# Sixty-four rows instead of fifty in the score products of an attention loop

## The chip, the cores and the metric

The kernel runs on one core of one Trainium2 chip. The metric is device time in microseconds (us) of one launch, here the median of three runs. The core has a matrix engine (TensorE, "PE"; its weight loads are listed apart as "PEld"), a vector engine (VectorE, "DVE"), an activation engine (ScalarE, "ACT"), GpSimd ("POOL") and SyncE ("SP"), which here only issues transfers (DMAs).

## The reference

Two mixers of the same sequence, blended by a gate. Sequence 2048, width 512, 32 heads of 16. The second mixer reads an input of its own name with the same values, so the kernel takes one `x`.

```python
g = sigmoid((x * gate_w).sum(-1, keepdims=True))
# a: full softmax attention
qkv = (x @ wqkv).reshape(B, S, 3, H, Dh).transpose(2, 0, 3, 1, 4)
scores = einsum("bhqd,bhkd->bhqk", q, k) * Dh ** -0.5
a = (softmax(scores) @ v, heads joined) @ wo
# b: Fourier mixing with given matrices, real part
b = dft_seq_re @ (x @ dft_hid_re.T) - dft_seq_im @ (x @ dft_hid_im.T)
out = g * a + (1 - g) * b
```

The weights `wqkv` and `wo` are drawn 64 times larger than usual, so the scores are large and the softmax needs the maximum of each row of scores.

## The kernel before

**Number format.** Products run in a 32-bit format of reduced mantissa (`F32R`). Where that isn't exact enough, a number is split into a high and a low part, and three products (high-high, high-low, low-high) are added. For queries and keys this is done by stacking: a head of 16 becomes 48 rows, `[k hi, k hi, k lo]` against `[q hi, q lo, q hi]`, so one product of 48 rows gives the sum of the three.

**Two heads at a time.** A pair of heads `p` (16 pairs) lies in two tiles of 128 partitions, `qs` and `ks`, each 2048 wide: head 0 of the pair in partitions 0 to 47, head 1 in 64 to 111. `row_loads` (L84) makes the pair of tiles and its eight transfers. All these tiles come from the pool `stk`, which has six buffers; a transfer into a buffer waits until its last reader is done.

**Two passes.** The *scan* computes every score once to get the row maxima: `scan` (L121, product at L130, maximum on DVE at L132) or `scan_folded` (L136, products at L149). There are 64 scan steps a pair, 1024 in all. `shift` (L158) negates and splits the maxima of a pair into two rows and stores them in DRAM (`m_d`). The *use* pass loads a pair again with `load_use` (L103): after the eight row loads it fills, for each half `j`, two more rows from partition `b = 64*j + 48` on. The rows of `ks` get ones, from the DRAM tile `ones_d`; the rows of `qs` get the two rows of negated maxima. A product over 50 rows is thus the score less its maximum, and ACT can take the exponential straight from PSUM.

**The front** (the first 695 us) does the projections, the transform along the width, most of the transform along the sequence, and beside these the first 692 scan steps. At its start it loads `xT` and the weights through SP's queue (L414 to L422), then stores the ones to `ones_d` (L429), and goes on with stores of the projected queries and keys (L383, L215). Operands of the transforms are split into tiles `b0` to `b31` of the pool `big`; `block(i)` names them, and block 31 holds the low part of the last quarter of the last row block of `x`.

**The loop** (L893 on, the last 1050 us) has 16 pairs of 32 steps. A step handles 128 keys for 1024 queries of both heads: `qk2` (L634) makes the scores of 512 queries (`c = 0`: both heads into one pair of banks `s3`, one exponential of 1024 columns, L649) and of 512 more (`c = 1`: two single banks of three, two exponentials of 512 columns, L653). In each, the two heads are two products, one on each half of the array's rows (L645). `pv` (L658) multiplies the exponentials of an earlier step with the values, four heads' parts side by side in the columns of the array (L660), into the bank `pvb`. Beside this stand:

- steps 0 to 331: one scan step each (`next_scan`), L130 and L132;
- steps 333 to 460: the rest of the transform along the sequence (`spectral`, L776). Its coefficients come through SP (`load_unit`, L765, two buffers), are split by DVE (`split_unit`, L772 and L773, two buffers of each part) and multiplied at L180;
- from step 461 on: the output projection and the blend (`mix_heads`, `take_in`, L754). From step 333 on, `pv` runs for two steps at once in every second step.

**Order.** Each engine runs its instructions in program order, written out by hand. At step 18 of a pair the loop emits `load_use` of the next pair (L898); 10 steps before a scan ends it emits the loads of the next scan. SP takes its transfers strictly one after the other. Each of them raises one of eight semaphores in turn, and waits until the transfer eight places before it has landed. The first score product of a pair waits for the transfers of its `qs` and `ks`.

Of the kernel before, what the change touches and what calls it, by code (L numbers as in the profile page):

```python
# [10 lines left out]
F32 = mybir.dt.float32  # L11
# [7 lines left out]
P = 128  # L19
S = 2048  # L20
D = 512
H = 32
DH = 16
# [23 lines left out]
def build(tc, x, xT, wqkv, wo, wrT, wiT, cr, ci, gate, out):  # L47
    nc = tc.nc
    with ExitStack() as ctx:
# [3 lines left out]
        big = ctx.enter_context(tc.tile_pool(name="big", bufs=1, reuse_waits="tile"))  # L53
        dram = ctx.enter_context(tc.tile_pool(name="dram", bufs=1, space=DRAM))
# [7 lines left out]
        y_d = [dram.tile([P, 4, D], F32, name=f"y_d{c}") for c in range(NC)]  # L62
        o_d = [[dram.tile([2, 2, NP // ND, 64, 512], F32, name=f"o_d{f}_{i}") for i in range(2)] for f in range(ND)]
        r_d = [[dram.tile([4, 512], F32, name=f"r_d{p}_{h}") for h in range(2)] for p in range(NP)]
        ones_d = dram.tile([2, S], F32, name="ones_d")

        ident = keep.tile([P, P], F32, name="ident")
        make_identity(nc, ident)
# [8 lines left out]
        gm = keep.tile([P, NB], F32, name="gm")  # L77
        ones = keep.tile([P, 32], F32, name="ones")
        nc.vector.memset(ones, 1.0)


        scanned, used, unfolded = {}, {}, {}

        def row_loads(p, queue, keys=k_d):  # L84

            qs = stk.tile([P, S], F32R, tag="stk", name="qs")
            ks = stk.tile([P, S], F32R, tag="stk", name="ks")
            loads = []
            for j in range(2):
                b, r = 64 * j, slice(DH * ((2 * p + j) % 8), DH * ((2 * p + j) % 8) + DH)  # L90
                loads += [(ks[b:b + 32, :], keys[p // 4][r, 0:1, :].to_broadcast([DH, 2, S])),
                          (qs[b:b + 32, :], q_d[p // 4][r, :, :].rearrange("e n s -> (e n) s")),
                          (ks[b + 32:b + 48, :], keys[p // 4][r, 1, :]),
                          (qs[b + 32:b + 48, :], q_d[p // 4][r, 0, :])]
            return (qs, ks), [lambda dst=dst, src=src: queue.dma_start(dst.bitcast(F32), src) for dst, src in loads]
# [7 lines left out]
        def load_use(p):  # L103
            if p < NP:
                used[p], loads = row_loads(p, nc.sync)
                for load in loads:
                    load()
                qs, ks = used[p]
                for j in range(2):
                    b = 64 * j + 48  # L110
                    nc.sync.dma_start(ks[b:b + 2, :].bitcast(F32), ones_d)
                    for n in range(2):
                        nc.sync.dma_start(qs[b + n:b + n + 1, :].bitcast(F32),
                                          m_d[p][n:n + 1, :, j].rearrange("n g b k -> n b g k"))
# [75 lines left out]
        with ExitStack() as pf:  # L190
# [126 lines left out]
            with ExitStack() as px:  # L317
# [94 lines left out]
                def load_x(c):  # L412
                    for d in range(ND):
                        nc.sync.dma_start(raws[d][:, q4[c]], xT[d * P:(d + 1) * P, q4[c]])  # L414
# [11 lines left out]
                load_x(2)  # L426
                load_cols(1, far)
                load_x(3)
                nc.sync.dma_start(ones_d.rearrange("a (b c) -> (a b) c", c=32), ones)  # L429
                gb = ep.tile([P, D], F32, tag="gb", name="gb", bufs=1)  # L430
                after(40, nc.sync.dma_start, gb, gate.to_broadcast([P, D]))

# [95 lines left out]
            with ExitStack() as py:  # L528
# [13 lines left out]
                pss, yre, early = {}, {}, {}  # L542
# [8 lines left out]
                for n, (ph, t, u) in enumerate(coef):  # L551
# [6 lines left out]
                    if n == len(coef) - 2 * NU:  # L558
                        unfolded[FRONT // SCANS], loads = row_loads(FRONT // SCANS, nc.sync)
                        for load in loads:  # L560
                            load()
                        load_use(0)
# [45 lines left out]
        with ExitStack() as pa:  # L608
# [18 lines left out]
            def bank():  # L627
                return ps2.tile([P, 512], F32, tag="s2", name="s2", bufs=3)

            def bank2():  # L630
                ps = ps2.tile([P, 2, 512], F32, tag="s3", name="s3")
                return ps, (ps[:, 0, :], ps[:, 1, :])

            def qk2(p, h, kb, c):  # L634
                n = turn[c]
                turn[c] += 1
                q0 = h * 1024 + c * 512
                qs, ks = used[p]
                if c == 0:
                    ps, pss = bank2()  # L640
                else:
                    pss = [bank() for j in range(2)]
                for j in range(2):
                    b = 64 * j
                    nc.tensor.matmul(pss[j], ks[b:b + 50, kb * P:(kb + 1) * P],  # L645
                                     qs[b:b + 50, q0:q0 + 512], start=True, stop=True)
                if c == 0:
                    e = both[n % len(both)]
                    nc.scalar.activation(e, ps, AF.Exp, scale=SCALE)  # L649
                    return [e[:, j, :] for j in range(2)]  # L650
                e = [ring[n % len(ring)] for ring in single]
                for j in (1, 0):
                    nc.scalar.activation(e[j], pss[j], AF.Exp, scale=SCALE)  # L653
                return e
# [238 lines left out]
            for step in range(NP * PERIODS):  # L893
                p, i = step // PERIODS, step % PERIODS
                h, kb = i // NB, i % NB
                now[0] = step
                if i == 18:
                    load_use(p + 1)  # L898
# [11 lines left out]
                if step >= MIX and step % 2 == 0:  # L910
                    next(fill)
                es = [qk2(p, h, kb, 0)]
                if step == 0:
                    es.append(qk2(p, h, kb, 1))
# [3 lines left out]
                if step:  # L918
                    es.append(qk2(p, h, kb, 1))
# [40 lines left out]
            c, ps = halves_[0], spread[0]  # L960
# [8 lines left out]
            c, ps = halves_[1], spread[1]  # L969
# [39 lines left out]
```

## Time and profile before

| what | value |
|---|---|
| median of three runs | 1755.48 us (1752.98 to 1757.93) |
| the profiled execution, its own time | 1751.4 us |
| its span, first to last instruction | 1749.6 us |
| mean granted TensorE clock | 0.995 |
| PE busy | 1719.9 us, 98% of the span |
| ACT busy | 1451.9 us, 83% |
| DVE busy | 1155.1 us, 66% |
| POOL busy | 712.7 us, 41% |
| transfers | 199.55 MB, mean 114 GB/s |

The profile is of one execution. A group's row gives the source line, the engine, the operation, the tiles written and read, the rows and columns of the array ("50*128"), the shape read, the count, the busy time (union) in us, the mean duration of one in ns, and the time that the engine stood idle before it with what ended that. Products overlap in the array and their ends are modelled, so the duration of one isn't the time that it takes from the next; the distance from start to start is. In a timeline a row is: start in us, length in us, engine, line, operation, tiles, count of merged instructions, and in brackets the idle time before it.

### The profile page before, as it was taken

How to read it: one execution, taken by the hardware profiler on the slowest of the kernel's cores; microseconds unless marked ns; L12 is line 12 of the kernel's file. 1: busy time of each engine (PE TensorE's matmuls, PEld its weight loads, DVE VectorE, ACT ScalarE, POOL GpSimd, SP SyncE). 2: the span in 40 equal slices, each digit the busy share in tenths (PEclk: the TensorE clock that was granted, in tenths of full speed). 3: DMA queues.
4: the chain of work that ended last, by engine and by line, in shares of the span. 5: the costliest groups of instructions: out<-in, count | busy, mean ns of one | idle time of the engine just before them, and what ended most of it. 6: DMA issues, size and time to landing. Idle time of an engine off the chain costs nothing.

```text
span 1749.6 us, 35589 instructions
## 1 busy us (share of the span) xinstructions
PE 1719.9 (98%) x13640; PEld 1021.8 (58%) x13640; DVE 1155.1 (66%) x1876; ACT 1451.9 (83%) x2384; POOL 712.7 (41%) x814
## 2 busy tenths in 40 slices
PE   8999999999999999999999999999999999999998
PEld 6887787888888887333333333333334555555554
DVE  6799999999999887666666666666664212222333
ACT  5445346888887887999999999999999888888885
POOL 3678667555556664032322323232232322322222
PEclk9999999999999999999999999999999999999999
DMA  8782666434354445433232423515313254255612
GB/s 296 254 298 79 190 201 206 121 115 117 104 154 140 139 133 120 74 59 63 58 67 56 82 40 64 95 23 99 78 35 73 64 118 90 68 141 137 177 36 100
DMA packets 126810, 199.55 MB, mean 114 GB/s; under 512 B 54016, under 2 KB 56560, under 8 KB 119728
## 3 DMA queue, kind: packets, MB, share of 16 engines
q1 hardware_dynamic: 84368, 161.02, 34.4%
q0 software_dynamic: 38496, 19.47, 5.2%
q10 hardware_dynamic: 3776, 16.78, 3.6%
q8 instruction: 107, 1.75, 0.4%
q14 instruction: 63, 0.52, 0.1%
HBM read 133.04 MB, written 63.71 MB: 112 GB/s over the span
## 4 chain that ended last, share of the span: by engine, by line
PE 89%; DMA 3%; DVE 3%; POOL 2%; issue 2%; ACT 1%; SPq 0%; DVEq 0%; ACTq 0%; POOLq 0%
PE pvb L660 28%; PE xy L180 21%; PE s L645 19%; PE s L180 8%; PE s L149 7%; PE s L130 6%; DVE mx L132 1%; DMA fa<-ks_d 1%; DMA kf_d<-fa 1%; POOL s L215 1%; DMA raws<-wqkv 0%; DMA raws<-xT 0%; POOL el L215 0%; POOL fa L215 0%; DMA abr<-ab_d 0%
## 5 line engine op out<-in xcount | busy, mean ns | idle before, releaser
L132 DVE TENSOR_REDUCE mx<-s 128x2 f32<-128x1024 f32 x524 | 627.2, 1222 | 207.5 <-PE s L130 207.4
L649 ACT ACTIVATE eb<-s 128x1024 f32<-128x1024 f32 x512 | 579.3, 1131 | 55.1 <-PE s L645 55.1
L653 ACT ACTIVATE e<-s 128x512 f32<-128x512 f32 x1024 | 610.3, 708 | 0.4 <-PE s L645 0.4
L660 PE MATMUL pvb<-e,va 128*17 128x512 f32 x2048 | 517.3, 598 | 0.0
L660 PE MATMUL pvb<-eb,va 128*17 128x512 f32 x2048 | 517.1, 598 | 0.0
L645 PE MATMUL s<-qs,ks 50*128 50x512 f32 x2048 | 428.1, 438 | 2.3 <-DVE ty L600 1.6
L645 PEld LDWEIGHTS s<-qs,ks 50*128 50x128 f32 x2048 | 212.6, 185 | 372.4 <-ACT eb L649 282.6
L155 DVE CUSTOM_DVE_ANT_0 fold<-s,fold 128x512 f32<-128x512 f32 x500 | 339.1, 690 | 39.0 <-PE s L149 19.4
L153 ACT ACTIVATE fold<-s 128x512 f32<-128x512 f32 x500 | 296.1, 602 | 70.0 <-PE s L149 43.1
L149 PE MATMUL s<-ks,qs 48*128 48x512 f32 x1000 | 223.3, 404 | 7.6 <-DVE mx L155 6.1
L130 PE MATMUL s<-ks,qs 48*128 48x512 f32 x1048 | 221.6, 396 | 3.7 <-DVE mx L132 2.5
L668 POOL DMA_DIRECT2D lc<-ob x124 | 63.1, 515 | 308.2 <-DVE ob L665 307.9
L660 PEld LDWEIGHTS pvb<-eb,va 128*17 128x17 f32 x2048 | 69.2, 96 | 190.2 <-issue 182.0
L149 PEld LDWEIGHTS s<-ks,qs 48*128 48x128 f32 x1000 | 120.9, 184 | 47.6 <-DVE mx L155 18.2
L675 POOL DMA_DIRECT2D r_d<-lc x31 | 18.1, 585 | 294.9 <-DVE lc L674 286.0
L130 PEld LDWEIGHTS s<-ks,qs 48*128 48x128 f32 x1048 | 108.3, 184 | 14.9 <-DVE mx L132 6.0
L180 PE MATMUL xy<-w,b 64*128 64x512 f32 x768 | 105.2, 392 | 0.2 <-ACT s L379 0.2
L401 ACT ACTIVATE tx<-xy 128x512 f32<-128x512 f32 x48 | 28.7, 599 | 78.6 <-PE xy L180 52.5
L754 DVE SCALAR_TENSOR_TENSOR y<-s,g,y 128x512 f32<-128x512 f32 x50 | 36.6, 748 | 76.6 <-PE s L180 76.0
L677 POOL DMA_DIRECT2D rb<-r_d x124 | 60.6, 496 | 63.0 <-DMA r_d<-lc 63.0
L180 PE MATMUL s<-b,chi 64*128 64x512 f32 x542 | 85.2, 390 | 0.3 <-ACT chi L963 0.3
L180 PEld LDWEIGHTS xy<-w,b 64*128 64x128 f32 x768 | 72.5, 186 | 17.6 <-ACT s L379 1.0
(750 smaller groups left out, 2320.4 us busy)
## 6 DMA issues: line engine op xcount, KB each, us to landing
craw<-ci SPq DMA_DIRECT2D x64, 256.0 KB
craw<-cr SPq DMA_DIRECT2D x60, 256.0 KB
ks<-k_d SPq DMA_DIRECT2D x46, 256.0 KB
qs<-q_d SPq DMA_DIRECT2D x46, 256.0 KB
ab_d<-ab SPq DMA_DIRECT2D x32, 256.0 KB
y_d<-y SPq DMA_DIRECT2D x32, 256.0 KB
o_d<-oh POOLq DMA_DIRECT2D x28, 256.0 KB, 9.8
o_d<-ol POOLq DMA_DIRECT2D x28, 256.0 KB, 11.9
```

The costliest lines, as they stand in the source:

```text
L130: nc.tensor.matmul(ps[:, j, :], qs[b:b + 48, qb * P:(qb + 1) * P], ks[b:b + 48, c * 512:(c + 1) * 512], start=True, stop=True)
L132: nc.vector.tensor_reduce(mx[p][:, :, qb, c], ps, axis=AX.X, op=ALU.max)
L149: nc.tensor.matmul(ps, qs[b:b + 48, qb * P:(qb + 1) * P], ks[b:b + 48, c * 512:(c + 1) * 512], start=True, stop=True)
L153: nc.scalar.activation(fold[j], ps, AF.Relu)
L155: nc.vector.tensor_tensor_reduce(out=fold[j], in0=ps, in1=fold[j], scale=1.0, scalar=-3.0e38, op0=ALU.add, op1=ALU.max, accum_out=mx[p][:, ...
L180: nc.tensor.matmul(ps[j], lhs[r], rhs[r], start=first, stop=last)
L645: nc.tensor.matmul(pss[j], ks[b:b + 50, kb * P:(kb + 1) * P], qs[b:b + 50, q0:q0 + 512], start=True, stop=True)
L649: nc.scalar.activation(e, ps, AF.Exp, scale=SCALE)
L653: nc.scalar.activation(e[j], pss[j], AF.Exp, scale=SCALE)
L660: nc.tensor.matmul(pvb[r:r + VC, :], va[:, kb, 2 * p + j, :], es[c][j], start=kb == 0, stop=kb == NB - 1, tile_position=(0, r))
L668: nc.gpsimd.dma_start(lc[32 * n:32 * n + 32, :], ob[r + DH:r + VC, :].rearrange("p (s e) -> p s e", e=16))
L677: nc.gpsimd.dma_start(rb[r:r + DH, :], r_d[p][h][n:n + 1, :].to_broadcast([DH, 512]))
```

## The change

The score products of the loop (L645) read 64 rows of `ks` and `qs` from partition `64*j` on, where they read 50. The 14 rows more are filled by `load_use`: in `ks` the transfer of two rows of ones becomes one of 16 rows of `ones_d`, whose last 14 are zeros; in `qs` a new transfer brings 14 rows of zeros. `ones_d` grows from 2 to 16 rows. A tile `zeros` is set to zero by DVE at the start, in the buffer of block 31, and one new transfer in the front writes it to the 14 rows.

```diff
-        ones_d = dram.tile([2, S], F32, name="ones_d")
+        ones_d = dram.tile([DH, S], F32, name="ones_d")
...
+        zeros = big.tile([112, S // 8], F32, tag="b31", name="zeros")
+        nc.vector.memset(zeros, 0.0)
...
                     b = 64 * j + 48
-                    nc.sync.dma_start(ks[b:b + 2, :].bitcast(F32), ones_d)
+                    nc.sync.dma_start(ks[b:b + DH, :].bitcast(F32), ones_d)
+                    nc.sync.dma_start(qs[b + 2:b + DH, :].bitcast(F32), ones_d[2:DH, :])
                     for n in range(2):
                         nc.sync.dma_start(qs[b + n:b + n + 1, :].bitcast(F32),
                                           m_d[p][n:n + 1, :, j].rearrange("n g b k -> n b g k"))
...
-                nc.sync.dma_start(ones_d.rearrange("a (b c) -> (a b) c", c=32), ones)
+
+                nc.sync.dma_start(ones_d[0:2, :].rearrange("a (b c) -> (a b) c", c=32), ones)
+                nc.sync.dma_start(ones_d[2:DH, :].rearrange("a (b c) -> (a b) c", c=S // 8), zeros)
...
                     b = 64 * j
-                    nc.tensor.matmul(pss[j], ks[b:b + 50, kb * P:(kb + 1) * P],
-                                     qs[b:b + 50, q0:q0 + 512], start=True, stop=True)
+                    nc.tensor.matmul(pss[j], ks[b:b + 64, kb * P:(kb + 1) * P],
+                                     qs[b:b + 64, q0:q0 + 512], start=True, stop=True)
```

`DH` is 16, `S` is 2048. The zeros add nothing to any score.

## The prediction

> **What bounds the kernel now.** I read the chain of work that ended last, then the groups that the change touches, then the busy times by stage, and last the timelines of single steps.
>
> ```profile
> PE 89%; DMA 3%; DVE 3%; POOL 2%; issue 2%; ACT 1%; SPq 0%; DVEq 0%; ACTq 0%; POOLq 0%
> ...
> L645 PE MATMUL s<-qs,ks 50*128 50x512 f32 x2048 | 428.1, 438 | 2.3 <-DVE ty L600 1.6
> L645 PEld LDWEIGHTS s<-qs,ks 50*128 50x128 f32 x2048 | 212.6, 185 | 372.4 <-ACT eb L649 282.6
> ...
> L130 PE MATMUL s<-ks,qs 48*128 48x512 f32 x1048 | 221.6, 396 | 3.7 <-DVE mx L132 2.5
> ...
> L180 PE MATMUL xy<-w,b 64*128 64x512 f32 x768 | 105.2, 392 | 0.2 <-ACT s L379 0.2
> ```
>
> PE leads the chain, and L645 stands there with 438 ns over 50 rows against 396 over 48 and 392 over 64. This looks as if 50 rows were a bad number. The trap is that this column is a modelled length of overlapping products; what counts is the distance from one pair of products to the next, and what stood before the pair. The loop has two stages:
>
> ```profile
> 720.00:1300.00 580.00, 580.00 (x4284) 218.97 (x4284) 392.45 (x365) 580.00 (x919) 176.44 (x264) 1.00 0.33 63
> 1330.00:1600.00 270.00, 270.00 (x2226) 143.86 (x2228) 57.29 (x99) 241.19 (x372) 73.75 (x110) 1.00 0.44 104
> ```
>
> The columns are the stretch, its length, busy us (with counts) of PE, PEld, DVE, ACT and POOL, the granted clock, the transfers' share and GB/s. With a scan step beside (first row) ACT is busy all the time, as PE is; later (second row) ACT has 29 us of slack in 270 and PE none. The clock is whole in both, so there is no throttle to win from. A step of the first stage:
>
> ```profile
> 902.31 0.50 PE L645 MATMUL s<-qs,ks 50*128 50x512 f32 x2
> 902.65 0.39 PE L130 MATMUL s<-ks,qs 48*128 48x512 f32 x2
> 902.85 1.24 ACT L649 ACTIVATE eb<-s 128x1024 f32<-128x1024 f32 x1
> 902.88 0.39 PE L645 MATMUL s<-qs,ks 50*128 50x512 f32 x2
> ...
> 904.20 0.50 PE L645 MATMUL s<-qs,ks 50*128 50x512 f32 x2
> 904.74 1.25 ACT L649 ACTIVATE eb<-s 128x1024 f32<-128x1024 f32 x1
> ```
>
> Here is a ring: the `c = 0` pair at 902.31, its exponential 0.54 us later, which ends at 904.09 and frees the only pair of banks, and the next `c = 0` pair at 904.20: 1.89 us a step. ACT's starts in this stage follow each other by at least 0.477 + 0.477 + 0.921 = 1.875 us, so ACT alone would allow only 0.015 us less. A step of the second stage, where PE has no gap:
>
> ```profile
> 1500.65 0.73 PE L645 MATMUL s<-qs,ks 50*128 50x512 f32 x4
> 1501.21 0.63 PE L180 MATMUL s<-b,chi 64*128 64x512 f32 x4
> 1501.68 0.40 PE L180 MATMUL s<-b,clo 64*128 64x512 f32 x2
> ...
> 1502.38 0.40 PE L180 MATMUL s<-b,clo 64*128 64x512 f32 x2
> 1502.61 0.63 PE L645 MATMUL s<-qs,ks 50*128 50x512 f32 x4
> ```
>
> Each pair, of 50 rows or 64, takes its 0.23 us, except the first after the value products (1500.65, two pairs in 0.56 us). The 0.50 us and the mean of 438 come from this place, not from the rows.
>
> **The change, part by part.**
>
> *The products.* Over all start times in the trace, the medians from a pair to the next are: a 48-row pair before a 50-row one 234 ns, 64 before 48 232, 48 before 64 235, 50 before 64 233, 64 before 50 233, 64 before 64 227 to 231. Right behind the value products the pair takes 337 ns with 50 rows, and 337 in the one place near the end where a 64-row pair stands there. Weight loads: 185 ns (50 rows), and 186 at L180 (64 rows). So a product costs by its 512 columns, and the array's half is occupied the same. There are 1024 pairs: 1024 x 0 = 0. The bounds: 50 before 50, in the odd steps of the second stage, takes 241 ns, and 64 before 64 at the least 227, so at best -14 ns a pair; on the other side the usual distances of 64-row pairs reach 237 against 230 for 50-row ones, +7 ns. On the path lie the `c = 0` pairs of the 332 scan steps (the ring) and both pairs of the other 180 steps: 332 + 360 = 692 pairs. That makes -9.7 to +4.8 us. I take 0, since the 241 stands only where the second weight load waits for ACT to free a bank.
>
> *The transfers of the loop.* Each `load_use` moves in each half 14 more rows of `ks` and 14 of `qs`, 8 KB a row: 56 rows, 448 KB, by two more transfers and two larger ones. While such loads run, the rows arrive at 104 to 216 KB per us (1548 to 1551 us), so the load takes 448/216 = 2.1 to 448/104 = 4.3 us longer; I take 3. Issue on SP is 0.4 us each, inside that. What hides it is the lead: the last row of maxima of a pair is issued 14.7 us or more before its first product (pair 0: 680.3 against 695.0; later 15.8 or more), and lands some 2 us on, by the median of the `rb` loads. Of 12.7 us, 3 are used. Pushed back behind it on SP's queue are the `yre` load and `y_d` stores at the front's end (POOL then waits 8.9 us for another tile anyway), scan loads, and in the second stage the coefficients:
>
> ```profile
> 1555.09 0.54 SPq L113 DMA_DIRECT2D qs<-m_d  x1
> ...
> 1556.95 1.06 SPq L765 DMA_DIRECT2D craw<-ci  x2
> ```
> ```profile
> 1354.67 0.43 DVE L772 CAST chi<-craw 128x512 fp32r<-128x512 f32 x1 [1.81 <-PE s L645]
> ...
> 1563.99 0.43 DVE L772 CAST chi<-craw 128x512 fp32r<-128x512 f32 x1 [5.88 <-PE s L180]
> 1564.52 0.69 DVE L773 TENSOR_TENSOR clo<-craw,chi 128x512 fp32r<-128x512 f32 x1
> ```
>
> This is the tightest cover. Casts fall every 8.74 us where PE sets them (1345.24, so 1353.98 would be due; 1555.03, so 1563.77): at both places the cast is already 0.2 to 0.7 us late, which says that the coefficient arrives just in time behind a `load_use`. Three us more go straight into DVE. But PE needs these parts only when the next block starts, at 1575.5 us for the second (the group of L180 after the one at 1571.16, 4.37 us on): 1575.5 - 1565.2 = 10.3 us of cover, and about 9.8 at the first. Of this 3 to 4.3 are used, and nothing else queues behind the cast that PE needs sooner. Cost 0. [...]
>
> *The front.* DVE's new memset of 112 x 256 lies between those of 128 x 32 (85 ns) and 128 x 512 (485 ns), so about 0.27 us, at 2.4 us, where DVE waits until 4.69 for the first `x`. The block 31 that it borrows is written only after 30 us, its transfer is read by then. The transfer itself stands on SP's queue behind `ones`, where the queue is full and PE pays:
>
> ```profile
> 19.80 0.32 SPq L215 DMA_DIRECT2D ks_d<-s  x1
> ...
> 25.85 0.73 PE L180 MATMUL xy<-b,w 64*128 64x512 f32 x4 [1.41 <-DVE b L282]
> ```
>
> The store of 19.80 lands at 24.38; DVE stands behind it, and PE behind DVE. The new transfer has 112 packets of 1 KB; such packets took 48 ns there, on 16 engines 112 x 48 / 16 = 0.34 us, and each later transfer waits for a neighbour one place on. From 0 to 0.34 + 2.75 (the longest step between two issues there, 22.45 to 25.20): I take 0.5.
>
> *Waits at the start of a pair.* L645 has 64 semaphore instructions of 51 ns, four a pair. The new count of 16 transfers behind eight semaphores changes them by one or two a pair at most: +-1.6 us, taken as 0.
>
> **Sum:** 0 + 0 + 0.5 + 0 on the profiled 1751.4 us is 1751.9. That execution lies 4.1 us under the median of 1755.5, so the forecast against the median is **1756.0 us**, no change that can be told (0.3%, or 5.3 us, is about what a measurement of this kernel can tell from no change). Its own range, with a few ns a pair either way and the front's bounds, is 1752 to 1760.
>
> **Rivals.**
>
> *A. The full half is faster.* If 227 ns holds for every pair in place of 241, 692 x 14 ns = 9.7 us, so 1746. For it: the 241, and the ring and PE leave no other slack. Against it: all mixed distances are 232 to 235, and ACT caps the ring at 0.015 us a step. Chance 0.17.
>
> *B. More rows cost PE time* (the other side). If the array takes 10 ns longer for 64 rows, the same 692 pairs cost 6.9 us, 1763. It counts as slower from 7.7 ns a pair on. For it: 237 and 235 are the longest usual distances. Against it: 48 to 64 rows within 3 ns. Chance 0.12.
>
> *C. Late coefficients.* If the two new transfers took as long as the `ks_d` store (4.59 us) and the two larger ones 1.3 more, `load_use` grows by 11.8 us; over 9.8, PE waits (11.8 - 9.8) at four places: 8 us, 1764. It decides from a growth of 9.8 us and is slower than 0.3% from 11.1. For it: the casts that are late already. Against it: measured rates. Chance 0.11.
>
> **How the numbers follow.** Forecast 0.60, A 0.17, B 0.12, C 0.11. So faster 0.17, within 0.3% 0.60, slower 0.23. The range 1748 to 1763 takes in the forecast's own, the nearer part of A, and B.
>
> **What would show it.** Right: L645 with 64 rows at 0.23 us from pair to pair and still 0.34 behind the value products; 1.89 us a step; coefficient casts behind a `load_use` some 3 us later with PE unmoved. A mean that falls from 438 with the distances unchanged would say nothing. Wrong: a ring under 1.88 us or odd steps shorter by 0.02 (A); pairs at 0.24 or more (B); PE at L180 idle, released by DVE `clo` L773 (C); PE idle at 25 us by more than 2 us (front).

## The result and the profile after

| | before | after |
|---|---|---|
| median of six runs, us | 1756.89 (1752.98 to 1758.38) | 1769.18 (1766.42 to 1771.85) |
| profiled execution, us | 1751.40 | 1768.51 |
| its span, us | 1749.6 | 1766.7 |

The changed kernel takes 1.0077 times as long, with a 95% interval of 1.0063 to 1.009: by this ratio 13.5 us more (the medians of the table lie 12.3 apart). No change had been forecast, and 1769.18 lies above the range given. In the profiled executions it is 17.1 us. Line numbers are two to five higher than before: L645 is now L650, L674 is L679, L130 and L132 are L133 and L135, L180 is L183.

From the page of the changed kernel, the shares of the chain of waits and three of the groups:

```profile
PE 83%; DMA 7%; DVE 4%; POOL 2%; issue 2%; ACT 1%; SPq 0%; DVEq 0%; ACTq 0%; POOLq 0%
PE pvb L665 25%; PE xy L183 22%; PE s L650 16%; PE s L183 8%; PE s L152 7%; PE s L133 6%; DMA lc<-ob 5%; DVE mx L135 2%; DMA raws<-xT 1%; POOL lc L673 1%; POOL s L218 1%; POOL el L218 0%; DMA fa<-ks_d 0%; DVE ob L670 0%; DMA abr<-ab_d 0%
...
L650 PE MATMUL s<-qs,ks 64*128 64x512 f32 x2048 | 428.3, 438 | 2.3 <-DVE ty L605 1.6
L650 PEld LDWEIGHTS s<-qs,ks 64*128 64x128 f32 x2048 | 207.0, 185 | 375.3 <-ACT eb L654 275.0
...
L133 PE MATMUL s<-ks,qs 48*128 48x512 f32 x1048 | 223.4, 398 | 18.2 <-DVE mx L135 17.0
```

The product that was changed is as it was: 438 ns and 428 us, with 64 rows as with 50. What is new stands beside it. DMA went from 3% to 7% of the chain, and 5% is one small transfer, `lc<-ob`; the scan product L133 has 18.2 us of idle PE ahead of it where it had 3.7, nearly all put down to DVE's maxima. The loop's two stages, in the columns of the prediction (busy PE, PEld, DVE, ACT and POOL, clock, transfers' share, GB/s):

```profile
720.00:1300.00 580.00, 566.53 (x4138) 205.71 (x4138) 378.51 (x351) 561.73 (x887) 170.44 (x256) 0.99 0.38 71
1330.00:1600.00 270.00, 270.00 (x2208) 140.57 (x2208) 62.33 (x100) 242.92 (x376) 74.82 (x108) 1.00 0.43 101
```

In the second stage PE still has no gap (270.00 us busy of 270). In the stage with scans PE lost 13.5 us in 580, ACT 18, and the clock is a little short of whole. So the loss lies there. The waits of that stretch (total us, times, longest), before:

```profile
DVE lc L674 <- DMA lc<-ob: 2.3, 5, 0.8
PEld s L130 <- DVE mx L132: 0.3, 1, 0.3
```

and after:

```profile
DVE lc L679 <- DMA lc<-ob: 20.4, 9, 4.8
PEld s L133 <- DVE mx L135: 15.7, 7, 4.3
PE s L133 <- DVE mx L135: 13.4, 6, 3.9
```

At the end of a half of a pair, DVE copies the sums into `ob` (L670), POOL gathers the row sums into `lc` by four small transfers (L673, 64 bytes a piece), and seven steps later DVE takes their reciprocal (L679). DVE waits for this gather in the kernel before too, but in this stretch for 0.8 us at most; now up to 4.8. One such place in DVE's timeline (start, length, and in brackets the idle time ahead with what ended it), before:

```profile
772.23 1.23 DVE L132 TENSOR_REDUCE mx<-s 128x2 f32<-128x1024 f32 x1 [0.66 <-PE s L130]
773.67 0.25 DVE L674 RECIPROCAL lc<-lc 128x16 f32<-128x16 f32 x1 [0.20 <-DMA lc<-ob]
774.12 1.23 DVE L132 TENSOR_REDUCE mx<-s 128x2 f32<-128x1024 f32 x1 [0.20 <-PE s L130]
```

and after, with PE's timeline of the same place under it:

```profile
769.45 1.23 DVE L135 TENSOR_REDUCE mx<-s 128x2 f32<-128x1024 f32 x1 [0.65 <-PE s L133]
773.66 0.25 DVE L679 RECIPROCAL lc<-lc 128x16 f32<-128x16 f32 x1 [2.98 <-DMA lc<-ob]
773.83 1.16 DVE L135 TENSOR_REDUCE mx<-s 128x2 f32<-128x1024 f32 x1
```
```profile
772.45 0.51 PE L650 MATMUL s<-qs,ks 64*128 64x512 f32 x2
775.04 0.50 PE L133 MATMUL s<-ks,qs 48*128 48x512 f32 x2 [2.09 <-DVE mx L135]
```

The maxima of the scan that should follow at about 771.3 stand behind the reciprocal on DVE until 773.83. PE's next scan product needs the banks that they free, and stands until 775.04; behind it stand the score products, and the ring. The chain of waits of the changed kernel, in order of time, says what the reciprocal waited for:

```profile
757.51 0.70 DVE ob L670
...
758.49 1.52 POOL lc L673 x3
760.01 13.52 DMA lc<-ob
...
773.66 0.25 DVE lc L679
773.91 1.09 DVE mx L135
775.04 0.50 PE s L133 x2
```

The gather is issued at 760.01 and lands 13.5 us on. Where no load runs beside it, 1.7 us from the last issue to the reciprocal is enough (1716.64 to 1718.30, at the end). Beside it here, on SP's queue:

```profile
754.50 0.56 SPq L97 DMA_DIRECT2D ks<-k_d  x1
...
762.49 0.30 SPq L113 DMA_DIRECT2D ks<-ones_d  x1
763.71 0.31 SPq L114 DMA_DIRECT2D qs<-ones_d  x1
...
770.60 1.36 SPq L116 DMA_DIRECT2D qs<-m_d  x2
```

This is the `load_use` with the added rows, over the whole time of the gather. The tiles for these rows come free at the end of a pair; in this stage such a load falls at the start of pairs 1, 3, 5, 7 and 9, when POOL gathers the sums of the second half of the pair before. (In the middle of the even pairs such a load and a gather meet too; the waits there are 0.9, 0.3, 1.2 and 0.5 us.) On POOL's own queue two stores of 256 KB stand ahead of the gather:

```profile
749.73 0.88 POOL L696 DMA_DIRECT2D o_d<-oh  x1
750.60 0.82 POOL L696 DMA_DIRECT2D o_d<-ol  x1
```

At the five places the second of them lands 17.3 to 18.6 us after its issue before the change and 18.0 to 19.9 after it, so at most a part of the gather's delay comes through the stores. From its last issue to its landing the gather takes 10.5 to 11.3 us at these places before and 13.3 to 15.3 after. Beside the load of a scan, which the change leaves as it was (start of pairs 2, 4, 6 and 8), it takes 9.5 to 9.8 and 9.2 to 10.1 us; with no load beside it (middle of pairs 1 to 9, the odd ones) 2.7 to 3.7 and 1.6 to 2.9.

At the five places of the two profiled executions:

| start of pair | DVE's wait ahead of the reciprocal, before, us | after, us | lost there, us | granted clock then halved |
|---|---|---|---|---|
| 1 | 0.2 | 3.0 | 3.8 | yes |
| 3 | 0.3 | 3.3 | 2.6 | no |
| 5 | 0.0 | 2.8 | 3.7 | yes |
| 7 | 0.8 | 4.8 | 5.5 | yes |
| 9 | 0.6 | 3.6 | 4.4 | yes |

"Lost" is how much the distance between the two executions grew over the place, by the starts of the exponentials of L654. The five make 20.0 us. Up to the loop the changed kernel's execution was ahead by 2.8 us (the one before has a dip of the clock of 6.8 us at 696), and 20.0 - 2.8 = 17.2 is the distance at the end. It is 17.1 at step 320 and 17.2 at step 511: the second stage gives and takes nothing.

### The profile page after: what moved, and what is told of

Its sections match the earlier page's. It is cut to its first block, busy times and chain, and to the rows that moved or that the text cites. A ratio compares the mean times of both kernels' runs of the same rounds, so it can differ in the third digit from the quotient of the medians.

```text
span 1766.7 us, 35624 instructions
## 1 busy us (share of the span) xinstructions
PE 1723.5 (98%) x13640; PEld 1016.2 (58%) x13640; DVE 1152.8 (65%) x1877; ACT 1452.7 (82%) x2384; POOL 711.4 (40%) x814
## 3 DMA queue, kind: packets, MB, share of 16 engines
q1 hardware_dynamic: 86288, 168.48, 36.4%
## 4 chain that ended last, share of the span: by engine, by line
PE 83%; DMA 7%; DVE 4%; POOL 2%; issue 2%; ACT 1%; SPq 0%; DVEq 0%; ACTq 0%; POOLq 0%
PE pvb L665 25%; PE xy L183 22%; PE s L650 16%; PE s L183 8%; PE s L152 7%; PE s L133 6%; DMA lc<-ob 5%; DVE mx L135 2%; DMA raws<-xT 1%; POOL lc L673 1%; POOL s L218 1%; POOL el L218 0%; DMA fa<-ks_d 0%; DVE ob L670 0%; DMA abr<-ab_d 0%
## 5 line engine op out<-in xcount | busy, mean ns | idle before, releaser
L135 DVE TENSOR_REDUCE mx<-s 128x2 f32<-128x1024 f32 x524 | 626.2, 1221 | 206.3 <-PE s L133 206.1
L654 ACT ACTIVATE eb<-s 128x1024 f32<-128x1024 f32 x512 | 569.5, 1112 | 60.5 <-PE s L650 60.4
L658 ACT ACTIVATE e<-s 128x512 f32<-128x512 f32 x1024 | 599.8, 688 | 11.2 <-PE s L650 11.2
L650 PE MATMUL s<-qs,ks 64*128 64x512 f32 x2048 | 428.3, 438 | 2.3 <-DVE ty L605 1.6
L650 PEld LDWEIGHTS s<-qs,ks 64*128 64x128 f32 x2048 | 207.0, 185 | 375.3 <-ACT eb L654 275.0
L133 PE MATMUL s<-ks,qs 48*128 48x512 f32 x1048 | 223.4, 398 | 18.2 <-DVE mx L135 17.0
L152 PE MATMUL s<-ks,qs 48*128 48x512 f32 x1000 | 228.0, 404 | 7.4 <-DVE mx L158 6.1
L673 POOL DMA_DIRECT2D lc<-ob x124 | 63.0, 515 | 293.4 <-DVE ob L670 293.0
L133 PEld LDWEIGHTS s<-ks,qs 48*128 48x128 f32 x1048 | 108.7, 184 | 32.2 <-DVE mx L135 23.4
L183 PE MATMUL xy<-w,b 64*128 64x512 f32 x768 | 105.3, 392 | 0.2 <-ACT s L382 0.2
L183 PE MATMUL s<-b,chi 64*128 64x512 f32 x542 | 85.7, 391 | 0.3 <-ACT chi L968 0.3
L183 PEld LDWEIGHTS xy<-w,b 64*128 64x128 f32 x768 | 72.5, 186 | 17.5 <-ACT s L382 1.0
## 6 DMA issues: line engine op xcount, KB each, us to landing
o_d<-ol POOLq DMA_DIRECT2D x28, 256.0 KB, 12.8
```

Of the source, the lines that this page charges most:

```text
L133: nc.tensor.matmul(ps[:, j, :], qs[b:b + 48, qb * P:(qb + 1) * P], ks[b:b + 48, c * 512:(c + 1) * 512], start=True, stop=True)
L135: nc.vector.tensor_reduce(mx[p][:, :, qb, c], ps, axis=AX.X, op=ALU.max)
L152: nc.tensor.matmul(ps, qs[b:b + 48, qb * P:(qb + 1) * P], ks[b:b + 48, c * 512:(c + 1) * 512], start=True, stop=True)
L183: nc.tensor.matmul(ps[j], lhs[r], rhs[r], start=first, stop=last)
L650: nc.tensor.matmul(pss[j], ks[b:b + 64, kb * P:(kb + 1) * P], qs[b:b + 64, q0:q0 + 512], start=True, stop=True)
L673: nc.gpsimd.dma_start(lc[32 * n:32 * n + 32, :], ob[r + DH:r + VC, :].rearrange("p (s e) -> p s e", e=16))
```

## The experiments

The theory to be tested (T): the added rows keep the transfer engines busy longer (their share of the 580 us went from 0.33 to 0.38) just when POOL's gather must pass them; the gather lands late; DVE, and behind it the scan and PE, wait. The rival (R): a product over 64 rows costs PE more.

**The transfers without the products.** The loop's products read 50 rows again; all added rows are still brought.

```diff
-                    nc.tensor.matmul(pss[j], ks[b:b + 64, kb * P:(kb + 1) * P],
-                                     qs[b:b + 64, q0:q0 + 512], start=True, stop=True)
+                    nc.tensor.matmul(pss[j], ks[b:b + 50, kb * P:(kb + 1) * P],
+                                     qs[b:b + 50, q0:q0 + 512], start=True, stop=True)
```

> The changed kernel with score products of 50 rows again; all its transfers stay, so 14 rows of each half are loaded and not read. Theory T (the added rows arrive on SP's queue while POOL's four gathers of the row sums, lc, are under way; the gathers land some 3 us later; DVE's reciprocal waits for them, the scan maxima wait behind it, and the ring of products and exponentials stops): as slow as the changed kernel, ratio to before 1.0065 to 1.009, with DVE idle in front of the reciprocal at the same five places. Theory R (64 rows cost PE time): same as before, ratio 1.000 within 0.002.

Measured: 1767.63 us, 1.0074 (1.0053 to 1.0095) times the kernel before. The loss is whole with 50 rows. Its waits, over the whole execution, the second stage with them:

```profile
DVE lc L679 <- DMA lc<-ob: 37.3, 13, 6.5
```

After the change it was 40.3 us, 13 times, and in the kernel before 15.8 us, 9 times. At the five places DVE waits 2.4, 4.4, 2.6, 2.1 and 2.8 us. So R is not the cause of the loss.

**The same load, more time for the gather.** In the stage with scans the reciprocal is put ten steps after the copy where it was seven; once in the changed kernel, once in the kernel before.

```diff
-                    halved.append((step + (7 if done[0] < NP - 1 else 3), quotients(*done[:2])))
+                    halved.append((step + (3 if done[0] == NP - 1 else 10 if step < MIX else 7), quotients(*done[:2])))
```

> The changed kernel with the reciprocal and what follows it emitted 10 steps after the copy of the sums instead of 7, in the scan stage (before step 333); everything else, 64 rows and all transfers, as in the changed kernel. Theory T: the gather has 5.7 us more, the lateness of 3 to 5 us is covered, and the time goes back to that of before, 1753 to 1758, ratio 0.997 to 1.001; no DVE idle in front of the reciprocal in the scan stage. Theory R: as slow as the changed kernel, ratio 1.0065 to 1.009.

> The kernel before with the reciprocal 10 steps after the copy instead of 7 in the scan stage; the control of the run above. Theory T: the kernel before loses only 0.2 to 0.8 us at a few of these places (2.2 us in all), so 0 to 3 us are gained, ratio 0.998 to 1.000, and the one above stands within 2 us of this one. Theory R says nothing of this run; with it the one above would stand 12 us over this one.

Measured: the changed kernel with it 1754.37 us, 0.9997 (0.9986 to 1.0009); the kernel before with it 1752.48 us, 0.9999 (0.9987 to 1.0012). With 64 rows and every added transfer in place the loss is gone. DVE's timeline of the changed kernel with ten steps, at the place shown above:

```profile
777.28 1.23 DVE L135 TENSOR_REDUCE mx<-s 128x2 f32<-128x1024 f32 x1 [0.67 <-PE s L133]
778.43 0.24 DVE L679 RECIPROCAL lc<-lc 128x16 f32<-128x16 f32 x1
779.17 1.23 DVE L135 TENSOR_REDUCE mx<-s 128x2 f32<-128x1024 f32 x1 [0.50 <-PE s L133]
```

The reciprocal follows the maxima with no wait. So the added rows cost only through this wait, and 64 rows neither cost nor save more than about 0.15%, by the interval. The ten steps leave little room: at the tightest place the gather lands at 1264.60, and the reciprocal starts at 1264.72. The kernel before gains nothing from the longer lead: its waits of 0.8 us at most were hidden. No version tried is faster than the kernel before.

**The zeros at another time.** 64 rows; SP brings the two rows of ones as before the change, and POOL's queue brings the zero rows some steps into the pair, after its gather. Those of pair 0, ahead of the loop, stay on SP's queue.

```diff
-                    nc.sync.dma_start(ks[b:b + DH, :].bitcast(F32), ones_d)
-                    nc.sync.dma_start(qs[b + 2:b + DH, :].bitcast(F32), ones_d[2:DH, :])
+                    nc.sync.dma_start(ks[b:b + 2, :].bitcast(F32), ones_d[0:2, :])
...
+        def zero_rows(p, queue):
+            if p < NP:
+                for j in range(2):
+                    b = 64 * j + 48
+                    for t in used[p]:
+                        queue.dma_start(t[b + 2:b + DH, :].bitcast(F32), ones_d[2:DH, :])
...
+                if i == 20:
+                    zero_rows(p + 1, nc.gpsimd)
```

> 64-row products with the same zeros, but the loop's zero rows (14 of ks and 14 of qs in each half) are no longer on SP's queue behind the row loads: POOL issues them at step 20 of a pair, behind the gathers in its own queue; SP brings two rows of ones as before. Same bytes in all. Theory T: the gathers land as before, ratio 0.998 to 1.002. Theory R: as slow as the changed kernel, 1.0065 to 1.009. If the bytes themselves slow the loop wherever they lie, it is slow too, and then the run with 50 rows is slow as well.

Measured: 1757.31 us, 1.0024 (1.0013 to 1.0035), a little above what T gave. The waits at the five places are 0.2, 1.2, 0.9, 0.4 and 0.7 us, so these are nearly gone, with the same bytes. In the middle of even pairs, waits of up to 1.8 us come in their place. In the profiled execution 4.9 us were lost ahead of the loop and 3.1 in it. The part ahead of the loop says little: it was 4.3 us in an execution of the kernel before with another place of the reciprocal alone (the last run below), whose front is unchanged.

**Half of the added rows.** Products over 50 rows; the rows of zeros go to `ks` alone, so the added transfers of the loop are gone too.

```diff
                     nc.sync.dma_start(ks[b:b + DH, :].bitcast(F32), ones_d)
-                    nc.sync.dma_start(qs[b + 2:b + DH, :].bitcast(F32), ones_d[2:DH, :])
...
```

> Products of 50 rows; of the added transfers only the larger one of ks stays (16 rows of ones and zeros in place of 2), without the zero rows of qs: half of the added bytes, none of the added transfers in the loop. Theory T with a lateness that grows with the rows on SP's queue: gathers 1 to 2 us late at the same five places, 3 to 10 us lost, ratio 1.002 to 1.006. If it is the number of transfers that counts, same as before, ratio 1.000 within 0.0015; if any added row is enough, as slow as the changed kernel, 1.007 or more.

Measured: 1760.1 us, 1.0036 (1.0022 to 1.0051); waits of 1.7, 1.2, 0.7, 1.5 and 2.2 us (sum 7.3 against 14.3 with all rows and the same products), and no fall of the clock behind them. Half of the rows cost about half.

**One step more.** The changed kernel, the reciprocal eight steps after the copy.

```diff
-                    halved.append((step + (7 if done[0] < NP - 1 else 3), quotients(*done[:2])))
+                    halved.append((step + (3 if done[0] == NP - 1 else 8 if step < MIX else 7), quotients(*done[:2])))
```

> The changed kernel with the reciprocal 8 steps after the copy of the sums instead of 7 in the scan stage: 1.9 us more for the gather. Theory T: of the five waits of 2.8 to 4.8 us 0.9 to 2.9 are left, so 3 to 9 us are lost, ratio 1.002 to 1.005; the waits in front of the reciprocal shrink by 1.9 us each. If what helped at 10 steps was another place in DVE's order and not the lead, the ratio is 1.000 or 1.0075, not between.

Measured: 1762.33 us, 1.0031 (1.001 to 1.0053). The ratio is in T's bounds, but the waits of the profiled execution, 0.1, 2.8, 1.8, 2.9 and 2.3 us, are not all a step (1.9 us) shorter: the sum falls from 17.5 to 9.9, where 8.0 would be left of these waits less a step each. The times scatter from 1750.6 to 1768.5 us: how late the gather lands seems to differ from one execution to the next. In the middle of the even pairs the waits even grew, from 0.9, 0.3, 1.2 and 0.5 to 1.3, 1.8, 0.8 and 1.5 us. One reason stands in the traces, and was not tested by itself: POOL's two stores follow the reciprocal, so with a later reciprocal they stand closer ahead of the next gather (in the changed kernel, at the place shown above, the second store is issued at 750.60 and the gather from 758.49 on; a step is 1.9 us). Beside the load of a scan, which has no added row, the gather takes 12.2 to 12.8 us here, against 9.2 to 10.1 in the changed kernel. This run supports T only weakly.

**The rows in smaller pieces.** 64 rows, the same bytes at the same place; the added rows cross in pieces of 2 KB where a row went as one of 8 KB (`ones_d` is kept with a gap after each 512 numbers, and the front writes its ones and zeros in that shape).

```diff
-        ones_d = dram.tile([DH, S], F32, name="ones_d")
+        ones_p = dram.tile([DH, 4, 544], F32, name="ones_d")
+        ones_d = ones_p[:, :, 0:512]
...
-                    nc.sync.dma_start(ks[b:b + DH, :].bitcast(F32), ones_d)
-                    nc.sync.dma_start(qs[b + 2:b + DH, :].bitcast(F32), ones_d[2:DH, :])
+                    nc.sync.dma_start(ks[b:b + DH, :].rearrange("a (q c) -> a q c", c=512).bitcast(F32), ones_d)
+                    nc.sync.dma_start(qs[b + 2:b + DH, :].rearrange("a (q c) -> a q c", c=512).bitcast(F32), ones_p[2:DH, :, 0:512])
...
```

> The changed kernel with the added rows in pieces of 2 KB in place of whole rows of 8 KB (the DRAM tile of ones and zeros is padded, so that a contiguous run is 2 KB); 64 rows, same bytes, same places. If the gathers' small packets wait each for an 8 KB packet of SP's queue (theory P), the lateness shrinks to a half or less, ratio 1.001 to 1.005. If the bytes that go before count, as slow as the changed kernel, 1.0065 to 1.009. If four times as many pieces are themselves slower, slower still.

Measured: 1761.95 us, 1.0036 (1.0017 to 1.0056); waits of 1.0, 3.3, 2.3, 2.7 and 1.3 us, 10.7 in sum against 17.5. The number of bytes alone does not set the delay, their pieces do too. The interval is wide. The load itself is no shorter with them: at the five places it takes 17.0 to 18.6 us from its first issue to its last, against 16.9 to 19.2 in the changed kernel. So it looks as if the gather passes shorter pieces sooner; this rests on one execution of each.

**The loss without the change.** The kernel before, the reciprocal five steps after the copy in place of seven. No row is added.

```diff
-                    halved.append((step + (7 if done[0] < NP - 1 else 3), quotients(*done[:2])))
+                    halved.append((step + (3 if done[0] == NP - 1 else 5 if step < MIX else 7), quotients(*done[:2])))
```

> The kernel before, 50 rows and none of the added transfers, with the reciprocal 5 steps after the copy of the sums instead of 7 in the scan stage. Theory T says that the lead of the gather alone decides, so the loss can be had without any added row: 3.8 us of lead are gone, the waits of 0.2 to 0.8 us at five places grow to some 4 us and others may open, 10 to 25 us are lost, ratio 1.006 to 1.014. If the loss needs the added rows in some other way (their products, their place in memory, the clock), the ratio is 1.000 within 0.002.

Measured: 1769.66 us, 1.0082 (1.0061 to 1.0103), the loss of the change. Its waits in the stretch of 720 to 1300 us:

```profile
DVE lc L674 <- DMA lc<-ob: 23.2, 14, 3.1
PEld s L130 <- DVE mx L132: 15.5, 12, 2.6
```

They look like those of the changed kernel: at the five places 3.0, 3.1, 3.1, 2.5 and 3.0 us. So the gather's lead decides, and seven steps were just enough for the loads of the kernel before: there the gather of pair 1 was issued at 762.80 and used at 773.67, 10.9 us on, of which 0.2 were a wait. The 13.5 us of the changed kernel do not fit into that.

## Why the prediction was wrong

The failed step is **the transfers of the loop**. Their size was about right: 3 us more were taken for a `load_use`, and at the five places it takes 2.1 to 4.7 us more from its first issue to its last (14.4 to 15.1 before, 16.9 to 19.2 after). The gather that passes it at the start of pair 1 lands 13.5 us after its issue, 2.8 later than at the same place before (10.7, of the 10.9 to the reciprocal). What failed is the list of what waits for it. The prediction counted the load's own first use (12.7 us of cover), and what is "pushed back behind it on SP's queue". POOL's gather stands on no queue of SP's, and so was never listed. Its cover had been used up: the wait of L674 for `lc<-ob` stood in the profile of before, five times in the stage, 0.8 us at most, and no row of the prediction looked at it. The cost of 0 was in truth about 20 us in the profiled loop. That the rows on SP's queue delay this gather all the same, the trace shows: the gather on POOL's queue of the changed kernel lands after 1.6 us where nothing runs beside it (at the end), after 1.6 to 2.9 with POOL's own stores ahead of it and no load, and after 13.3 to 15.3 with SP's rows beside it too. How they delay it the traces do not show. That both queues load the same transfer engines is an estimate from the page of the changed kernel, which counts both as shares of 16 engines: 36.4% for the queue with SP's transfers (q1), 5.1% for the one with POOL's (q0).

Point by point:

- **The products, 0.** Right. With the lead lengthened, 64 rows take 0.9997 of the time of 50. In the second stage of the changed kernel, PE's timeline:

```profile
1500.43 0.73 PE L650 MATMUL s<-qs,ks 64*128 64x512 f32 x4
1501.00 0.62 PE L183 MATMUL s<-b,chi 64*128 64x512 f32 x4
1501.46 0.39 PE L183 MATMUL s<-b,clo 64*128 64x512 f32 x2
...
1502.38 0.65 PE L650 MATMUL s<-qs,ks 64*128 64x512 f32 x4
```

  The first pairs still take 0.57 us for two behind the value products, the others 0.23. The 241 ns of an odd step's first pair did fall to 231, as rival A had it, but the next distance rose from 336 to 348: the place only moved.
- **The ring, 1.89 us a step.** Right outside the five stalls: between 720 and 1300 us the starts of L654 follow each other by 1.885 us in the median (L649 before: 1.890), close to ACT's bound of 1.875.
- **The front, 0.5 us.** Neither shown nor refuted. In the profiled executions the store of `ks_d` went from 19.80 to 20.60, the product from 25.85 to 26.44 (+0.59). But with the front unchanged the same product starts at 25.59 in one of the other traces (the kernel before with ten steps) and at 26.48 in another (with five), so that the 0.59 can be chance.

```profile
20.60 0.32 SPq L218 DMA_DIRECT2D ks_d<-s  x1
...
26.44 0.73 PE L183 MATMUL xy<-b,w 64*128 64x512 f32 x4 [2.49 <-DVE b L285]
```

- **Late coefficients** (and rival C). The lateness came as said, and more of it. DVE's waits of the whole execution for them, before and after:

```profile
DVE chi L772 <- DMA craw<-ci: 1.6, 1, 1.6
```
```profile
DVE chi L777 <- DMA craw<-ci: 19.2, 6, 7.9
```

  PE stayed covered, as the constant distance of 17.1 to 17.2 us through the second stage shows. Rival C had the right kind of mechanism, a transfer late behind the longer load and an engine behind it, and its 1764 was nearest to the result; its place was wrong, and so was its limit of 9.8 us of growth. That its time came nearest is luck.
- **Rivals A and B** fell with the first two experiments. Of the signs named for a wrong forecast, the ring under 1.88 us, pairs at 0.24 us and PE idle for `clo` did not come. The sign for the front came, PE idle at 25 us by more than 2 us (2.49), but it tells nothing: with the front unchanged PE was idle there for 1.26 us in one trace and 2.07 in another. What the loss showed itself by, PE idle for the scan's maxima, was not among the signs.

The time itself: by the ratio 13.5 us are to be explained, in the profiled pair 20.0 in five stalls. The stalls differ between executions, and only the profiled ones can be taken apart.

## What to carry to other kernels

When a change lengthens a transfer, list every small transfer of every queue that is under way in the same microseconds, not only those behind it on its own queue, and look up whether its consumer already waits for it in the profile of before: the wait of 0.2 us at the start of pair 1, which cost nothing, said that the cover was at zero, and became one of 3.0. What waits holds all that stands behind it on its engine (here 2.98 us of the reciprocal held the scan's maxima on DVE, and PE stood for 2.09), so its lead should be set with room for the longest load that can fall beside it. If more rows must be brought, the lead can be lengthened with them: three steps more removed the whole loss here. A longer lead moves what follows the wait too (here POOL's stores), and this may delay the next small transfer: with one step more the gather beside the load of a scan took 12.2 to 12.8 us where it had taken 9.2 to 10.1, though that the stores did it was not tested by itself.

## What the hardware showed unasked

After four of the five stalls of PE, of 2 to 4 us, the granted clock halved for 3.41 us (from 776.55 to 779.96 after the first of them, at 0.50). The windows over and after the stall shown above, for the changed kernel (the last three columns are clock, transfers' share and GB/s):

```profile
773.00:776.00 3.00, 0.96 (x8) 0.43 (x12) 1.75 (x3) 1.40 (x3) 0.59 (x1) 1.00 0.03 3
776.00:780.00 4.00, 4.00 (x22) 0.99 (x14) 2.04 (x2) 2.92 (x5) 2.00 (x5) 0.57 0.12 37
```

PE works 0.96 us of the first 3, and then issues 22 products in 4 us at a clock of 0.57, where the kernel before issued 34 in these 4 us. Idle times of 2.09, 1.98, 2.69 and 3.94 us were followed by a fall, one of 2.42 was not; in the run with the transfers alone 1.52, 1.71 and 3.46 were, 1.20 and 1.96 were not. A place with a fall loses 0.7 to 0.9 us more than DVE waited, one without 0.6 to 0.8 less (the table, and the run with the transfers alone): some 1.5 us for a fall, near the half of 3.41. So by this estimate four falls make about 6 of the 20 us. The length of the idle time alone does not decide over a fall: in the changed kernel 1.98 us sufficed in one place, and 2.42 did not in another. The falls of the changed kernel's loop begin at 776.55, 1025.72, 1152.02 and 1278.31 us, 73, 37 and 37 times 3.413 us apart, and the trace gives each a length of 3.413 us. So their beginnings may lie on a grid of that length; this is an estimate from these four times. Whether the place of an idle time in this grid decides over a fall stays open.
